# Attention and a gated MoE block on one core: 245 offsets in the plan that orders its work

## The chip, the cores and the metric

The kernel runs on one core of a Trainium2 chip. Its time is the device time of one execution in microseconds. The profile and the trace record one execution on the same core; a time "at 42 us" counts from the first instruction of that execution.

## The reference: what is computed

Eight batches, twelve heads, 448 positions, head size 64. Queries and keys are normalised and scaled by a gain, attention runs without a mask, and the heads side by side (448 x 768 per batch) go through a gated block that mixes positions.

```python
def rmsnorm(x, g):
    return x / np.sqrt(np.mean(x * x, axis=-1, keepdims=True) + 1e-06) * g
q_n, k_n = rmsnorm(q, g_q), rmsnorm(k, g_k)
scores = (1 / np.sqrt(64)) * q_n @ k_n.transpose(0, 1, 3, 2)
attn = np.exp(scores - max)                 # softmax over the keys
x = (attn / sum) @ v                        # -> (8, 448, 768)
h = np.maximum(x @ w_in, 0.0)               # 768 -> 1024
u, v = h[..., :512], h[..., 512:]
v_n = (v - mean(v)) / np.sqrt(var(v) + 1e-06)
v_s = np.einsum('ts,bsd->btd', w_spatial, v_n) + b_spatial[None, :, None]
out = (u * v_s) @ w_out                     # 512 -> 768
```

## The kernel before: tasks, a planner, five engines

The kernel doesn't write its instructions in the order in which they run. It makes a list of 1178 tasks, each with its engine or engines, a duration that the author assumes for each, the tasks it depends on, the buffers it takes and a **position** (`pos`): the smaller, the sooner it is wanted. A planner then walks through assumed time and takes, for one engine after the other, the task that goes next. What comes out is one fixed instruction order per engine; on the chip each engine runs its list strictly in that order and waits where an input or a buffer isn't there yet.

```python
def add(self, *a, **k):
    t = Task(*a, **k)
    ...
    t.pos += self.nudge.get(t.name, 0.0)            # NUDGE["exp G3 r5"]: an offset to the position
    for e in t.costs:
        if f"{t.name} @{e}" in self.nudge:          # NUDGE["relu_u1 b0 @ACT"]: a bias for one engine
            t.bias = {**t.bias, e: self.nudge[f"{t.name} @{e}"]}

# in run(): among the tasks of an engine that could start soon
    for at, t in c:
        if at > first + self.LOOK[e]:
            continue
        if len(t.costs) > 1:                        # two engines can do it: the one that ends first
            mine = at + t.costs[e][1] + t.bias.get(e, 0.0)
            if any(self.start_of(t, o) + t.costs[o][1] + t.bias.get(o, 0.0) < mine - 1e-6
                   for o in t.costs if o != e):
                continue
        s = t.pos + self.WAIT * (at - first)
        if e == "PE" and t.mode != mode:            # TensorE: changing the shape of the array
            s += self.KEEP                          # 0.6; the plan also charges SWITCH = 0.095 for it
        if top is None or (s, at) < top[0]:
            top = ((s, at), t, at)
```

The work comes in 24 groups G (a batch has three: four heads each). Each group is loaded, squared, reduced, scaled, turned (transposed), scored in seven rounds, and each round's scores go through an exponential on ScalarE. From the exponentials TensorE forms the row sums and the values, which VectorE divides into `xt`. When a batch b has its three groups, its gated block runs: `unit_v`, `unit_u`, `unit_s`, `unit_o`. Names as in the plan:

```python
# square{i} G / reduce{i} G / rstd G / scaled{i} G : norm of q (i=0) and k (i=1)
costs = {"POOL": (1.65 * w, ...)}                   # square: GpSimd, and for the first 8 groups
if early: costs["ACT"] = ...; costs["DVE"] = ...    # ScalarE or VectorE as well
# turn{i} G: by TensorE into PSUM for G < 6 (then turned{i} G copies it out, on DVE or ACT);
#            by a transposing DMA from group 6 on (then k_scale G, on DVE or ACT)
# scores [(G, r)]: 8 matmuls of 64x64 tiles, four side by side; blocks of two rounds from G3 on
add(f"scores {blk}", {"PE": ...}, pos, emit, deps=..., get=bufs, mode="S")
# exp G r
act.activation(out=eb.t[:, r], in_=bf.t[:, :, 0:S], func=AF.Exp, bias=0.0, scale=1.0)
# sums G / values0 G / values1 G: matmuls of 128x32 tiles, four side by side, mode "V"
# recip G (ACT: Ln, then Exp), xt0 G / xt1 G (DVE: values times reciprocal)
# w_spT0..3: w_spatial is turned once, by 49 TensorE transposes of 64x64, mode "S"
a = add(f"w_spT{c}", {"PE": (0.7, 1.0)}, 34.0, emit, deps=[wsp_load], get=[bf], mode="S")
# the gated block of batch b; mode "G" (128x128), and "O" for the last 64 positions
add(f"unit_v{c} b{b} {j0}", {"PE": (w, w + 0.26)}, pos, ..., mode="G" if c < 3 else "O")
a = add(f"relu_v{c} b{b}", {"DVE": (0.62, 0.73), "ACT": (0.49, 0.63)}, ...)
# stats{c} b (DVE), ln_rstd b (ACT), ln_apply{c} b (DVE)
# unit_u{f} b -> relu_u{f} b (DVE or ACT);  unit_s{f} b -> gate{f} b (DVE)
# unit_o{c}{h} b -> osb{c}{h} b (DVE or ACT) -> store{c} b (DMA)
```

Until about 25 us the planner also puts dummy matmuls (128x128, results unused) into gaps of TensorE.

Of the kernel before, what the change touches and what calls it, by code (L numbers as in the profile page):

```python
# [225 lines left out]
def kernel(  # L226
# [60 lines left out]

    plan = Planner(tc, NUDGE)
    add = plan.add
# [499 lines left out]


LOG = None
NUDGE = {}


# [28 lines left out]
```

## Time and profile before

| | us |
|---|---|
| time, median of 3 runs (lowest to highest) | 287.81 (287.23 to 288.43) |
| span of the profiled execution | 285.4 |
| TensorE matmul busy | 267.1 |
| ScalarE busy | 217.5 |
| VectorE busy | 209.8 |
| GpSimd busy | 157.2 |

TensorE (PE) is the fullest engine. Of the others ScalarE (ACT) and VectorE (DVE) come next, each about three quarters full over the whole span; over single stretches they are much fuller. The busy time of PE holds stretches in which several matmuls run side by side in different parts of the array, and their ends are modelled, so it says where PE was never empty, not how well it was used. For that, the distance from the start of one matmul to the start of the next is the better measure; the prediction uses it.

### The profile page before, as it was taken

What the parts mean: (1) busy time and instruction counts of PE and PEld (TensorE: products, weight loads), DVE (VectorE), ACT (ScalarE), POOL (GpSimd) and SP (SyncE); (2) the same over time, 40 slices, a digit from 0 to 9 for tenths busy, and PEclk for the clock granted to TensorE, in tenths of its full rate; (3) what the DMA queues carried; (4) which work ended last, traced back from release to release, by engine and by line L of the source; (5) the groups of instructions that cost most, each with busy time, mean ns of one, the idle gap of its engine ahead of it and who ended that gap; (6) DMA issues with size and microseconds to landing.
All of it is one profiled execution on the core that took longest, in us unless ns stands there. A gap on an engine that the chain in (4) does not pass through costs nothing.

```text
span 285.4 us, 7162 instructions
## 1 busy us (share of the span) xinstructions
PE 267.1 (94%) x2870; PEld 124.8 (44%) x2870; DVE 209.8 (74%) x357; ACT 217.5 (76%) x348; POOL 157.2 (55%) x132
## 2 busy tenths in 40 slices
PE   5688979999899999999999999999999999999990
PEld 5443436444344344444444443444443443445550
DVE  1999797889998858878888776874977667452530
ACT  4189984787877898878999887888887978876531
POOL 7533364965786498479888989149871440000011
PEclk9999997999999999999999999999999999999998
DMA  7999598387799978999898899988993562006114
GB/s 253 290 250 223 139 256 209 66 163 198 196 204 245 224 108 218 222 280 208 311 178 204 179 220 244 138 256 192 190 195 32 105 167 54 2 0 165 31 39 155
DMA packets 65379, 50.02 MB, mean 175 GB/s; under 512 B 41985, under 2 KB 61906, under 8 KB 65346
## 3 DMA queue, kind: packets, MB, share of 16 engines
q1 hardware_dynamic: 51266, 40.61, 57.4%
q0 software_dynamic: 14080, 8.96, 23.5%
q8 instruction: 22, 0.36, 0.6%
q14 instruction: 11, 0.09, 0.1%
HBM read 38.55 MB, written 11.01 MB: 174 GB/s over the span
## 4 chain that ended last, share of the span: by engine, by line
PE 66%; issue 19%; DVE 7%; ACT 3%; POOL 2%; POOLq 0%; DVEq 0%
PE pss L550 11%; PE ps L618 10%; PE ps L713 10%; PE ps L660 8%; PE ps L753 7%; PE ps L729 7%; PE ps L597 5%; ACT et L573 2%; PE ps L664 2%; DVE ms L462 2%; DVE sq L449 1%; PE ps L320 1%; DVE nq L483 1%; PE ps L774 1%; POOL nk L483 1%
## 5 line engine op out<-in xcount | busy, mean ns | idle before, releaser
L573 ACT ACTIVATE et<-pss 128x896 bf16<-128x896 f32 x168 | 144.2, 914 | 26.5 <-PE pss L550 25.8
L462 DVE TENSOR_REDUCE ms<-sq 128x14 f32<-128x896 f32 (+1 forms) x50 | 51.3, 1037 | 5.9 <-ACT sq L447 3.8
L550 PE MATMUL pss<-qT,kT 64*64 64x448 bf16 x672 | 51.3, 363 | 3.9 <-ACT et L573 2.5
L483 POOL TENSOR_TENSOR nq<-qf,rs 128x896 bf16<-128x896 f32 x17 | 28.7, 1689 | 39.6 <-ACT rs L470 29.5
L627 DVE TENSOR_TENSOR xt<-ps,rc 128x448 bf16<-128x448 f32 x48 | 29.0, 622 | 20.7 <-ACT rc L606 10.3
L618 PE MATMUL ps<-et,vt 128*32 128x448 bf16 x768 | 41.2, 353 | 0.1
L449 POOL TENSOR_TENSOR sq<-qf 128x896 f32<-128x896 f32 x20 | 33.7, 1685 | 12.2 <-DVE nk L483 4.1
L713 PE MATMUL ps<-xt,w_in 128*128 128x448 bf16 x192 | 39.9, 353 | 0.0
L449 POOL TENSOR_TENSOR sq<-kf 128x896 f32<-128x896 f32 x19 | 32.0, 1686 | 9.1 <-DVE sq L449 4.0
L483 POOL TENSOR_TENSOR nk<-kf,rs 128x896 bf16<-128x896 f32 x20 | 33.8, 1689 | 5.7 <-DVE nq L483 3.4
L660 PE MATMUL ps<-w_in,xt 128*128 128x512 bf16 x144 | 35.3, 384 | 0.1
L753 PE MATMUL ps<-w_out,gt 128*128 128x384 bf16 x192 | 34.7, 327 | 0.5 <-DVE gt L734 0.5
L550 PEld LDWEIGHTS <-kT 64*64 64x64 bf16 x672 | 15.0, 104 | 34.9 <-issue 29.8
L685 DVE BATCH_NORM_STATS2 s<-vs 128x6 f32<-128x512 bf16 (+1 forms) x32 | 22.0, 687 | 9.6 <-ACT vs L635 9.0
L729 PE MATMUL ps<-w_spT,vn 128*128 128x448 bf16 (+1 forms) x128 | 27.6, 354 | 0.0
L618 PEld LDWEIGHTS <-vt 128*32 128x32 bf16 x768 | 19.4, 97 | 18.0 <-issue 5.1
L734 DVE TENSOR_TENSOR gt<-ps,us 128x448 bf16<-128x448 f32 x32 | 19.8, 622 | 9.8 <-PE ps L729 8.5
L765 POOL DMA_DIRECT2D out_dram<-osb x3 | 1.7, 556 | 44.9 <-ACT osb L741 44.9
L713 PEld LDWEIGHTS <-w_in 128*128 128x128 bf16 x192 | 17.3, 98 | 20.6 <-issue 6.4
L375 POOL DMA_DIRECT2D vt<-in_v_dram x32 | 21.6, 683 | 6.2 <-DVE nq L483 3.2
L753 PEld LDWEIGHTS <-gt 128*128 128x128 bf16 x192 | 17.4, 98 | 16.9 <-issue 5.3
L597 PE MATMUL ps<-et,ones 128*32 128x448 bf16 x384 | 23.4, 355 | 0.3 <-ACT et L573 0.3
(69 smaller groups left out, 278.8 us busy)
## 6 DMA issues: line engine op xcount, KB each, us to landing
qf<-in_q_dram SPq DMA_DIRECT2D x24, 448.0 KB, 4.5
kf<-in_k_dram SPq DMA_DIRECT2D x24, 448.0 KB, 5.4
out_dram<-osb SPq DMA_DIRECT2D x45, 192.0 KB, 3.5
vt<-in_v_dram POOLq DMA_DIRECT2D x16, 192.0 KB, 6.6
vt<-in_v_dram POOLq DMA_DIRECT2D x16, 144.0 KB, 6.3
w_in<-in_moe_w_in_dram POOLq DMA_DIRECT2D x2, 768.0 KB, 9.2
out_dram<-osb SPq DMA_DIRECT2D x15, 96.0 KB, 3.2
w_out<-in_moe_w_out_dram POOLq DMA_DIRECT2D x1, 768.0 KB, 9.2
```

What stands on the lines that cost most here:

```text
L449: eng_of[e].tensor_tensor(out=sqb.t[:, h], in0=r.t[:, h], in1=r.t[:, h], op=ALU.mult)
L462: dve.tensor_reduce(out=ms.t[:, i, h], in_=sqb.t[:, h].rearrange("p a (s d) -> p a s d", d=D), axis=AX.X, op=ALU.add)
L483: eng_of[e].tensor_tensor(out=nb.t.rearrange("p s a d -> p a s d")[:, :, s0:s1, :], in0=r.t.rearrange("p a (s d) -> p a s d", d=D)[:, :, s ...
L550: pe.matmul(out=ps[64 * h:64 * h + 64, a, 0:S], lhsT=kb[64 * a:64 * a + 64, slot, 64 * xk:64 * xk + 64], rhs=qb[64 * a:64 * a + 64, :, 64 ...
L573: act.activation(out=eb.t[:, r], in_=bf.t[:, :, 0:S], func=AF.Exp, bias=0.0, scale=1.0)
L597: pe.matmul(out=bf.t[32 * l:32 * l + 32, 0:S], lhsT=ones[:, (0 if c < 3 else 1 + x), :], rhs=eb.t[:, r, a, :], start=(c == 0), stop=(c == ...
L618: pe.matmul(out=bf.t[32 * l:32 * l + 32, 0:S], lhsT=vb.t[:, 2 * (g + 3 * a) + x, c, half::2], rhs=eb.t[:, r, a, :], start=(c == 0), stop=( ...
L627: dve.tensor_tensor(out=xb.t[:, j * S:j * S + S], in0=bf.t[:, 0:S], in1=rc.t, op=ALU.mult)
L660: pe.matmul(out=bf.t, lhsT=xb.t[:, j * S + 128 * c:j * S + 128 * c + 128], rhs=w_in[:, j, DH:DF], start=(j == 0), stop=(j == 5))
L713: pe.matmul(out=bf.t[:, 0:S], lhsT=w_in[:, j, 128 * f:128 * f + 128], rhs=xb.t[:, j * S:j * S + S], start=(j == 0), stop=(j == 5))
L729: pe.matmul(out=bf.t[:, 0:S], lhsT=vn.t[0:kp, c, 128 * f:128 * f + 128], rhs=w_spT[0:kp, c, :], start=(c == 0), stop=(c == 3))
L753: pe.matmul(out=bf.t[:, 0:384], lhsT=gt.t[:, f, 128 * c:128 * c + 128], rhs=w_out[:, f, 384 * h:384 * h + 384], start=(f == 0), stop=(f == 3))
```

## The change

The table of offsets, empty before, is filled: 245 entries, of which 183 move a task's position (from -54 to +84) and 62 bias a task towards or away from one engine. It is the outcome of a search over plans, and it is for a better order of the same work: no task is added, removed or resized, and no result changes its arithmetic other than by the engine that evicts or squares it.

```diff
-NUDGE = {}
+NUDGE = {
+    "unit_o00 b5": 2, "unit_v1 b3 0": 0.3, "relu_u1 b1": 10, "unit_u1 b6": 11, "turn0 G3 0": -16,
...
+    "turned0 G0 0 @DVE": 7, "scores [(15, 2), (15, 3)]": -1, "square1 G4 0 @DVE": 3,
...
+    "values0 G23 0": 9, "values0 G22 0": 18, "unit_u2 b6": 5,
+    "osb00 b1 @ACT": -2, "scaled0 G9 0": 9, "rstd G19": 5, "w_spT1": -18, "values0 G3 0": 7,
...
+    "turn0 G5 0": 66, "sums G4 0": 45, "unit_o3 b4": -22, "exp G19 r0": -3, "reduce1 G10 0": 10,
+    "w_spT2": -54, "scaled1 G2 0": 4, "ln_apply0 b5": 7, "values0 G20 0": 3, "gate1 b0": -18,
...
+    "scaled0 G1 0 @POOL": -9, "square0 G1 0 @DVE": 11, "unit_v2 b5 0": 5.87032,
+    "scores [(13, 2), (13, 3)]": -13, "unit_v0 b0 4": -20, "square1 G10 0": 23,
+}
```

What it does to the order of instructions, read from the two built programs:

| | before | after |
|---|---|---|
| TensorE matmuls, of which dummies | 2869, 95 | 2867, 93 |
| changes of TensorE's array shape between two matmuls | 222 | 236 |
| tasks that change their engine | | 73 |
| `relu_u` on DVE / ACT | 23 / 9 | 15 / 17 |
| `osb` on DVE / ACT | 27 / 29 | 35 / 21 |
| `turned` on DVE / ACT | 14 / 0 | 9 / 5 |
| `scaled` on DVE / POOL | 13 / 37 | 10 / 40 |
| `square` on ACT / DVE / POOL | 5 / 6 / 39 | 7 / 7 / 36 |

Where TensorE meets the first gated block, the order before is: values of group 2, `w_spT0`, two rounds of scores, `w_spT1` to `w_spT3`, the rest of `unit_v0`, `unit_v3`, and on. After it is: `w_spT2` ahead of the last round of group 2, `w_spT1` between its sums, `w_spT0` and `w_spT3` between its values, then `unit_v1`, scores, the rest of `unit_v0` and `unit_v1`, `unit_v3`, `unit_u3`, `unit_v2`, the other `unit_u` with the turns of groups 4 and 5 between them, and only then the last round of group 3.

## The prediction, written before the changed kernel was run

> **What bounds the kernel now.** I read the page's slices of the span first (40 slices of 7.1 us; each digit a busy share in tenths).
>
> ```profile
> PE   5688979999899999999999999999999999999990
> ACT  4189984787877898878999887888887978876531
> PEclk9999997999999999999999999999999999999998
> ```
>
> PE is full from the twelfth slice on. Before that it has an 8 and a 7, ACT is at 9 in slices 4 and 5, and the granted clock dips in slice 7. So there are at least two regimes. Cutting the span at the first exponential, at the first gated block and at the end of group 5's values gives the table of stretches:
>
> ```profile
> 0.00:14.40 14.40, 8.97 (x99) 7.37 (x99) 8.01 (x23) 4.90 (x9) 9.59 (x22) 1.00 1.01 273
> 14.40:42.00 27.60, 23.27 (x327) 11.34 (x327) 25.85 (x31) 25.68 (x39) 10.92 (x12) 1.00 0.95 217
> 42.00:77.20 35.20, 33.81 (x375) 17.17 (x369) 30.48 (x49) 25.65 (x44) 22.30 (x17) 0.95 0.73 169
> 77.20:285.40 208.20, 201.04 (x2082) 88.89 (x2078) 145.50 (x257) 161.26 (x258) 114.39 (x84) 1.00 0.80 164
> ```
>
> (After each stretch and its length: busy us of PE, weight loads, DVE, ACT, POOL; clock; DMA share; GB/s.) From 14.4 to 42 ACT works 25.68 of 27.6 us and DVE 25.85: exponentials and norms set the pace, and PE has too little to do, because no gated block can run before group 2's values. From 77.2 on ACT has 161 of 208 us and PE never rests. What ended PE's waits there is one line of the list of waits, and the same list for 45 to 77.2 has two:
>
> ```profile
> PE ps L753 <- DVE gt L734: 0.5, 2, 0.3
> ...
> PE pss L550 <- ACT kT L527: 0.9, 1, 0.9
> PE ps L597 <- ACT et L573: 0.3, 1, 0.3
> ```
>
> But "never rests" isn't "at its peak". The starts of the matmul records show it: inside a run, 448 columns follow at 189 ns, 512 at 216, 384 at 163; where the array's shape changes, the next start is 282 ns away. PE's timeline shows it in the large:
>
> ```profile
> 99.52 0.57 PE L550 MATMUL pss<-qT,kT 64*64 64x448 bf16 x8
> 100.02 1.47 PE L753 MATMUL ps<-w_out,gt 128*128 128x384 bf16 x8
> 101.43 0.69 PE L550 MATMUL pss<-qT,kT 64*64 64x448 bf16 x8
> ```
>
> Eight score matmuls, four abreast, are 2 x 0.189 = 0.38 us, yet the next run starts 0.50 later. From 77.2 to the last matmul at 278.45 I added up all starts: 201.2 us elapsed; 181.1 us if each matmul took its distance within a run (four or two abreast counted once); 0.56 us in two waits; 161 shape changes. So a change costs (201.2 - 181.1 - 0.56)/161 = **0.122 us**, and 19.6 us of this stretch are changes. From 42 to 77.2 the same sum is 34.9 elapsed, 27.0 streamed, 24 changes at 0.122 = 2.9: **5.0 us lost**, to waits and clock. Where, the timeline tells:
>
> ```profile
> 42.78 2.28 PE L412 MATMUL ps<-ident,w_sp 64*64 64x64 bf16 x35 [0.23 <-DVE xt L627]
> 45.00 1.04 PE L660 MATMUL ps<-w_in,xt 128*128 128x512 bf16 x2
> ...
> 72.82 0.38 PE L550 MATMUL pss<-qT,kT 64*64 64x448 bf16 x4
> 74.09 0.38 PE L550 MATMUL pss<-qT,kT 64*64 64x448 bf16 x4 [0.89 <-ACT kT L527]
> ...
> 45.00:48.30 3.30, 3.30 (x23) 1.90 (x23) 2.30 (x5) 0.76 (x2) 1.69 (x1) 0.50 0.94 302
> ```
>
> While the gated block is ready (xt at 42.7), PE turns w_spatial until 45.0. Then the clock record grants half speed from 44.9 to 48.3, so the first matmuls of the block take twice their time: 1.7 us lost. At 72.8 to 75.4 scores wait for a k_scale on ACT, and sums for an exponential: 1.4 us.
>
> **What the Trainium skill says.** "TensorE: Matmul & The Clock Gate", Part 1, section "What's actually happening": the clock is halved or full, decided over free-running windows of 3.4 us by how busy PE was. The trace agrees: the half-speed record lasts 3.413 us and follows a window of short transposes with a 1.4 us gap. Its Part 4 says that transposes don't count as busy in the same way; that suits this place, though no run so far separates transposes from the gap. The section "Back-to-back issue gap" gives N/2.4 + 2.5 ns, 189.2 for 448 columns: 189 here. None of the three states the price of a shape change; the 0.122 is this trace's. "Perfetto Trace Analysis", section "Identifying the Most-Contended Engine", warns that matmul busy time misleads; here it reads 100% over a stretch with a tenth of it in changes.
>
> **The change part by part.**
>
> (1) *Start.* The square of k of group 1 moves from DVE (1.08 us, from 9.35 to 10.43) to ACT, and the first piece of the turned q of group 0 (0.42 us on DVE) moves to ACT. DVE scales group 0 as soon as ACT has its factor (10.05 instead of 10.35), and its chain of copies to the first scores is 0.42 shorter: first exponential 0.3 + 0.42 = **0.7 us** earlier, about 13.6.
>
> (2) *14 to 42 us.* ACT gets one more copy (a turned q of group 3, about 0.9 us by its 0.914 us for an exponential of 896 columns), DVE loses work. ACT stays the bound, and with 1.9 us of idle time in 27.6 there is little to win. I take group 2's values as ready at the same 42 us, or up to 0.7 earlier.
>
> (3) *w_spatial.* Its 49 transposes, 57 ns apart, are 2.8 us. About 40 of them stand after 42 us now. In the order after, all four tasks stand ahead of group 2's last values, between scores that wait for ACT. That takes **2.3 us** out of the full stretch, and spreads them so that a half-speed window becomes unlikely: **1.7 us**.
>
> (4) *First gated block.* PE does unit_u of batch 0 ahead of the last round of group 3, while ACT takes their four evictions (0.545 each), four turned copies and a square. Counted from the lists of tasks up to the last exponential of group 5, ACT gains 7.3 us of work and gives away 4.4 (k_scale, three osb, a relu_v3, two rstd): 3 us more. From 14.4 to 75.35 it now works 49.5 and idles 11.5, so it fits. In the order after, k_scale of group 6 is DVE's: the 1.4 us of waits at 73 should shrink; I count **0.7**.
>
> (5) *Shape changes.* 222 become 236. Up to the round that begins group 6 there are 5 more of them between tasks (56 for 51), where PE partly waits anyhow, and 7 more after it: 7 x 0.122 = **0.9 us lost**.
>
> (6) *The rest.* After 77 us there are only 0.56 us of waits to save. Last matmul to end of span (278.45 to 285.4) is one eviction on ACT and the last store; both stay: 0. DVE gets the osb back and sheds relu_u; neither engine bounds there.
>
> Sum if all goes well: -0.7 - 2.3 - 1.7 - 0.7 + 0.9 = -4.5 us, and -5.5 with the rest of the waits gone. The bound by PE agrees: streamed work after 42 us is 27.0 - 2.3 + 181.1 = 205.8, with some 196 changes at 0.122 = 23.9; from 41.5 that ends at 271.2, with 7.0 of tail a span of 278.2, or 7.2 less. No plan of many in-order lists reaches a bound of no wait at all. I take 80% of the 4.5, because the moved values and scores of groups 3 to 5 sit close to their exponentials: **-3.6 us**, 284.2.
>
> **Rivals.** *ACT becomes the bound in 44 to 77 us.* It is given 3 us, and six exponentials of 0.914 us sit behind evictions that PE itself waits for through four PSUM buffers. For it: ACT was at nine tenths before 42. Against it: 11.5 us of idle time. If it comes, parts 3 and 4 shrink to about half: -1.5, some 286.3. *A late stage that runs without waits now loses that.* Positions were moved by up to 36 far beyond batch 0, with no wait there to remove; values and first matmuls of the last block now follow each other directly. Every displaced pair could add a few tenths, 1 to 3 us in all: about 286. For it: the plan works with assumed durations; against it: the same durations gave a plan with 0.56 us of waits in 200. *Shape changes eat it.* With waits no smaller, 14 x 0.122 = 1.7 us slower, 289.5. Against it: the transposes visibly leave the full stretch. *More than I see.* The bound allows -7.2, 280.6, if the start and the waits vanish together.
>
> **Range and chances.** The parts are worth 1 to 6 us together; the rivals take up to 3. That gives 281.6 to 287.8 around **284.2**. Two per cent faster is 282.05, which needs nearly all of the bound: 0.17. Two per cent slower is 293.6, six us of new waits in a stage that has none: 0.02.
>
> **What would show it.** In the profile after: first exponential near 13.6; no w_sp transposes after the first unit_v of the full stretch, and clock 1.00 between 40 and 50 us; PE full from about 42; the last values of group 5 done three to four us before 77.2; from there on 201 us plus about 0.9 to the last matmul, and a tail of 7. It would be wrong if PE shows new waits for ACT or DVE after 77, if a half-speed window falls elsewhere, or if group 2's values come later than 42.

## The result, and the profile after

| | before | after |
|---|---|---|
| time, median (lowest to highest), us | 287.52 (287.18 to 288.43) | 284.31 (283.93 to 285.10) |
| ratio to before, 95% interval | | 0.9887 (0.9854 to 0.9920) |
| span of the profiled execution, us | 285.4 | 282.2 |

The change is 1.1% faster, about 3.2 us, and 284.31 stands beside 284.2 predicted. The page's slices of the span of the changed kernel, 7.05 us each:

```profile
PE   5788999899999999999999999999999999999990
ACT  4399998889977899798799889987887888773521
PEclk9999999999999999999999999999999999999997
```

The 7 in PE's sixth slice and the dip of the clock in the seventh are gone, and ACT stays at 8 or 9 in slices 6 and 7, where before it fell to 8 and 4. The stretches, cut at the same events as before (first exponential, first matmul of the gated block behind group 2's values, just behind the last values of group 5); after each stretch come the busy us of PE, weight loads, DVE, ACT and POOL, the clock, the DMA share and GB/s:

```profile
0.00:14.24 14.24, 9.45 (x95) 7.88 (x95) 6.92 (x21) 6.14 (x11) 9.51 (x22) 1.00 1.01 272
14.24:41.10 26.86, 24.33 (x354) 13.38 (x353) 23.96 (x30) 25.39 (x38) 15.73 (x14) 1.00 0.87 209
41.10:74.70 33.60, 32.39 (x356) 15.26 (x354) 29.62 (x47) 30.16 (x48) 17.66 (x13) 1.00 0.87 198
74.70:282.20 207.50, 199.58 (x2060) 88.20 (x2066) 146.67 (x252) 161.04 (x263) 115.54 (x84) 0.99 0.76 163
```

In the third stretch ACT now works 30.2 of 33.6 us; before it was 25.7 of 35.2. What ended PE's waits in that stretch, in the list of waits (us in total, times, longest):

```profile
PE pss L550 <- ACT qT L508: 0.9, 1, 0.9
PE pss L550 <- ACT et L573: 0.2, 1, 0.2
```

One wait for a copy on ACT has taken the place of another: 1.1 us here, 1.2 before. The wait for k_scale at 74 us is gone; the new one, for the turned q of group 4, ends at 53 us. PE's timeline where w_spatial is turned (L412) and the gated block begins (L660):

```profile
34.05 0.61 PE L412 MATMUL ps<-ident,w_sp 64*64 64x64 bf16 x10
...
35.66 0.91 PE L412 MATMUL ps<-ident,w_sp 64*64 64x64 bf16 x14
...
38.07 1.43 PE L412 MATMUL ps<-ident,w_sp 64*64 64x64 bf16 x19
...
41.13 1.04 PE L660 MATMUL ps<-w_in,xt 128*128 128x512 bf16 x3
...
42.60 1.04 PE L660 MATMUL ps<-w_in,xt 128*128 128x512 bf16 x4
```

The transposes are over when the block can go on: at 41.13 come matmuls that need only groups 0 and 1 (before has such at 30.96 already), and at 42.60 the first that need group 2, which before started at 45.00. The profile lacks eleven of the 144 matmul records of L660; gaps of 0.44 us between two of those are such holes and no waits.

For what follows I split every profile at three events: first exponential; start of the last values matmul of group 5; start of the last matmul. The first varies by a microsecond between profiles that start with the same instructions (14.24, 15.11 and 15.37 in three of them, 14.36 to 14.57 in five others), so the second column, counted from it, compares better than the span. What varies is the landing of a small transfer, the gains: in `after` VectorE's product of the gains starts behind it at 6.91 us, in w_spatial_back at 7.83 and in head_after at 8.09. In `after`, `tail_after` and the versions built on after, two rounds of scores of group 6 (0.50 us with their change of shape) fall ahead of the second event and not behind it.

| profile, us | first exponential | to group 5's last values | from there to the last matmul | to the end |
|---|---|---|---|---|
| before | 14.36 | 62.60 | 201.49 | 6.95 |
| after | 14.24 | 59.42 | 201.59 | 6.90 |
| head_after | 15.37 | 60.26 | 201.48 | 7.00 |
| tail_after | 14.37 | 63.22 | 201.34 | 6.82 |
| w_spatial_moved | 14.48 | 63.09 | 201.49 | 7.02 |
| w_spatial_by_matmul | 14.57 | 62.87 | 201.49 | 7.06 |
| w_spatial_back | 15.11 | 61.75 | 201.57 | 7.37 |
| engines_only | 15.78 | 69.69 | 201.30 | 6.99 |
| order_only | 15.57 | 68.87 | 201.57 | 6.76 |
| gains_later_before | 14.15 | 62.66 | 201.49 | 7.25 |
| k_scale_on_vector | 14.52 | 63.80 | 201.62 | 7.03 |
| gains_later | 12.55 | 59.50 | 201.56 | 7.02 |
| turns_sooner | 12.99 | 59.63 | 201.60 | 6.89 |
| turns_sooner_tail_before | 12.37 | 61.67 | 202.58 | 7.37 |

So the difference of 3.25 us between the two spans is 0.12 at the start, **3.18 between 14 and 77 us**, -0.10 in the 200 us after that, and 0.05 at the end. Counted at equal work, with the 0.50 us of the two rounds put back, it is 3.7 us gained up to group 5 and **0.6 us given back** in the late stage.

### The profile page after: what moved, and what is told of

The parts are those of the page before. It is cut to its first block, busy times and chain, and to the rows that moved or that the text cites. A ratio compares the mean times of both kernels' runs of the same rounds, so it can differ in the third digit from the quotient of the medians.

```text
span 282.2 us, 7121 instructions
## 1 busy us (share of the span) xinstructions
PE 265.8 (94%) x2857; PEld 124.7 (44%) x2868; DVE 207.2 (73%) x348; ACT 222.7 (79%) x357; POOL 158.4 (56%) x132
## 4 chain that ended last, share of the span: by engine, by line
PE 81%; ACT 7%; DVE 7%; POOL 2%; issue 2%; POOLq 0%; DVEq 0%; ACTq 0%
PE pss L550 14%; PE ps L753 12%; PE ps L618 11%; PE ps L660 10%; PE ps L713 10%; PE ps L729 9%; PE ps L597 7%; ACT et L573 4%; PE ps L664 2%; PE ps L774 2%; PE ps L320 2%; DVE s L685 1%; DVE nq L483 1%; PE ps L412 1%; DVE ms L462 1%
## 5 line engine op out<-in xcount | busy, mean ns | idle before, releaser
L483 POOL TENSOR_TENSOR nk<-kf,rs 128x896 bf16<-128x896 f32 x22 | 38.0, 1730 | 16.6 <-ACT rs L470 8.0
L618 PE MATMUL ps<-et,vt 128*32 128x448 bf16 x768 | 42.8, 354 | 0.0
L483 POOL TENSOR_TENSOR nq<-qf,rs 128x896 bf16<-128x896 f32 x18 | 30.4, 1692 | 17.8 <-ACT rs L470 8.0
L449 POOL TENSOR_TENSOR sq<-qf 128x896 f32<-128x896 f32 x18 | 30.3, 1684 | 13.2 <-DVE kT L529 8.1
L753 PE MATMUL ps<-w_out,gt 128*128 128x384 bf16 x192 | 35.2, 327 | 0.3 <-DVE gt L734 0.3
L660 PE MATMUL ps<-w_in,xt 128*128 128x512 bf16 x133 | 33.6, 380 | 1.0 <-issue 0.6
L449 POOL TENSOR_TENSOR sq<-kf 128x896 f32<-128x896 f32 x18 | 30.3, 1682 | 3.4 <-DVE ms L462 2.8
L765 POOL DMA_DIRECT2D out_dram<-osb x3 | 1.7, 557 | 48.3 <-ACT osb L741 48.3
L743 DVE COPY osb<-ps 128x384 f32<-128x384 f32 x35 | 18.6, 553 | 11.5 <-PE ps L753 11.1
```

The source lines that it names most:

```text
L449: eng_of[e].tensor_tensor(out=sqb.t[:, h], in0=r.t[:, h], in1=r.t[:, h], op=ALU.mult)
L483: eng_of[e].tensor_tensor(out=nb.t.rearrange("p s a d -> p a s d")[:, :, s0:s1, :], in0=r.t.rearrange("p a (s d) -> p a s d", d=D)[:, :, s ...
L618: pe.matmul(out=bf.t[32 * l:32 * l + 32, 0:S], lhsT=vb.t[:, 2 * (g + 3 * a) + x, c, half::2], rhs=eb.t[:, r, a, :], start=(c == 0), stop=( ...
L660: pe.matmul(out=bf.t, lhsT=xb.t[:, j * S + 128 * c:j * S + 128 * c + 128], rhs=w_in[:, j, DH:DF], start=(j == 0), stop=(j == 5))
L753: pe.matmul(out=bf.t[:, 0:384], lhsT=gt.t[:, f, 128 * c:128 * c + 128], rhs=w_out[:, f, 384 * h:384 * h + 384], start=(f == 0), stop=(f == 3))
```

## The experiments

With the offsets alone one can't try a part of the change: taking two of the 245 away makes the planner choose anew far behind. In the experiments the planner chooses nothing. It walks down a list of pairs (engine, task), written out from the order before or after, and each diff below is a diff of that list. Line numbers in these kernels stand 21 lower than in before and after.

```diff
-        for _ in range(len(self.tasks)):
-            ...                                # weigh the tasks, take the best
+        for e0, name in ORDER:                 # ("PE", "g2 col"), ("PE", "turn0 G0 0"), ...
+            at, e, t = self.start_of(named[name], e0), e0, named[name]
```

### Head or tail

**head_after**: the list of after up to the round that begins group 6, then the list of before for what is left.

> The order after up to the round that begins group 6 (to about 73 us), then the order before for all that is left; 219 changes of the array's shape between tasks instead of 226. Theory (the head carries the gain, 3.8 us at equal work, and the late moves cost 0.6): 283.7 us, the span from the last values of group 5 to the last matmul about 201.1. Rival (the late moves are needed to take up what the new head leaves behind): new waits of TensorE after 74 us, 285 to 286 us.

Measured 285.55 us, ratio 0.9899 (0.9874 to 0.9924): the head has nearly all of the gain. The 285.55 lies in the rival's range. Of the new waits that it named there is one, at 74.1 us at the joint, that neither order has (window 60 to 285 us of the list of waits):

```profile
PE ps L576 <- ACT et L552: 0.8, 1, 0.8
```

Behind it the third column is that of before (201.48), so the new head doesn't need the late moves. This profile also starts 1.1 us later than `after`, with the gains.

**tail_after**: the reverse, before up to that round, then after.

> The order before up to the same round, then the order after. Theory: 0.4 to 0.8 us slower than before, 288.1 us, for 7 more changes of the array's shape at 0.122 us. Rival (the late part holds a gain of its own): 287 us or less.

Measured 287.97, ratio 1.0003 (0.9988 to 1.0019). The late moves bring nothing, and cost less than expected: by the interval -0.3 to +0.5 us. The profile has 0.47 from the first exponential to the last matmul (264.56 for 264.09), within it.

### Moving w_spatial

**w_spatial_moved**: before, with eight tasks moved, and `bias` on DVE with them, right ahead of w_spT2's copy.

```diff
+PE  w_spT2          (ahead of scores (2,6); copies on DVE behind each)
+PE  w_spT1          (ahead of the second part of the sums of group 2)
+PE  w_spT0, w_spT3  (between the values of group 2)
-PE  w_spT0 ... w_spT3 (behind the values of group 2)
```

> The order before on every engine, with only the four tasks that turn w_spatial on TensorE, and their copies on VectorE, put where the order after has them, into the gaps between scores and values of group 2. Theory (2.3 us of transposes leave the full stretch and the half-speed window goes with them, 1.7 us): 283.8 to 285 us, clock 1.00 from 40 to 50 us. Rival (the gain is in the order of the first gated block and its evictions on ScalarE): at most 1 us faster, 286.5 to 287.5 us.

Measured 288.94, ratio 1.0031 (1.0014 to 1.0048): **slower**, and both expectations missed. The clock is full from 40 to 50 us, as the theory said. PE's timeline has the reason:

```profile
37.11 0.75 PE L576 MATMUL ps<-et,ones 128*32 128x448 bf16 x12 [0.84 <-DVE w_spT L397]
...
40.12 0.94 PE L597 MATMUL ps<-et,vt 128*32 128x448 bf16 x16 [0.77 <-DVE w_spT L397]
...
43.40 0.94 PE L597 MATMUL ps<-et,vt 128*32 128x448 bf16 x16 [0.47 <-DVE w_spT L397]
...
47.40 0.56 PE L478 MATMUL ps<-ident,nq 128*128 128x128 bf16 x7 [1.01 <-DVE nq L462]
...
49.23 0.56 PE L478 MATMUL ps<-ident,nk 128*128 128x128 bf16 x7 [0.83 <-ACT lnms L448]
```

The sums and values wait for a PSUM buffer that the copies of w_spatial free. The first two of these copies stand in DVE's list behind other work (`bias`, 0.95 us; a reduction and a square) while their transposes are done; the third follows its transposes at once. The gaps of PE were there, but DVE, 25.85 of 27.6 us full, had little room for what PE put into them. The last two waits, 1.84 us, are for the scaled q and k of group 4 (the second is listed under ACT, but GpSimd scales this k until 49.18). The scaling of q on DVE starts at 45.09 us for 44.04 in before, and takes 2.25 us for 1.08; a square on GpSimd ran beside its first 1.3 us, but whether that stretched it isn't shown. From unit_v3's first matmul to the scores at 73 us, at full clock, it is 27.89 us, where before takes 26.86 with 2.32 us of half speed in it. So this run gave back the clock's gain as well as that of the transposes.

**w_spatial_back**: the other way, after with these eight tasks put where before has them.

> The order after on every engine, with only the four tasks that turn w_spatial, and their copies, put back to where they stood before: behind the values of group 2, around the first matmuls of the gated block. Theory (in the order after they cost nothing and here they stand in the full stretch): 2.3 us slower than after, and up to 1.7 more if the half-speed window comes with them: 286.5 to 288 us. Rival (TensorE isn't what bounds the head, as moving them alone brought nothing): within 1 us of after, 284.3 to 285.3 us.

Measured 286.44, ratio 0.9970 (0.9951 to 0.9988), against 0.9887 of after: 0.83% or 2.4 us slower, and in the profile 2.33 us to group 5 (61.75 for 59.42). The 2.3 us of the expectation are there to the tenth, but that is partly luck: they were reckoned for some 40 transposes, and here all 49 stand in the full stretch again and take 3.0 us:

```profile
43.15 1.54 PE L391 MATMUL ps<-ident,w_sp 64*64 64x64 bf16 x28
44.62 1.04 PE L639 MATMUL ps<-w_in,xt 128*128 128x512 bf16 x4
45.59 1.63 PE L391 MATMUL ps<-ident,w_sp 64*64 64x64 bf16 x21
```

The clock record of this profile is at full speed until PE's work ends, so the half-speed window has no part in these 2.3 us, and 49 transposes in two rows need not bring it.

### The half-speed window

**w_spatial_by_matmul**: before, each transpose an ordinary matmul.

```diff
-pe.matmul(out=ps[64*y:64*y+64, t, 0:64], lhsT=x, rhs=ident[0:64, 0:64], is_transpose=True, ...)
+pe.matmul(out=ps[64*y:64*y+64, t, :], lhsT=x, rhs=ident[0:64, 0:64], start=True, stop=True)
```

> The order before, with the 49 transposes of w_spatial done as ordinary matmuls with the identity (float32 into PSUM), so that every instruction keeps its place. Theory (transposes don't count as work for the clock): no half-speed window at 45 us, 1.5 us faster, 286.0 us. Rival (the gap of 1.4 us ahead of them lowers the clock): the half-speed window stays, 287.5 us within 0.3.

Measured 287.81, ratio 1.0003 (0.9980 to 1.0026): no difference. The window didn't go; the clock record holds half speed for twice as long, from 42.0 to 48.9 us. So it isn't the kind of instruction, at least not alone. That the longer window cost only some 0.3 us (62.87 for 62.60) fits its place: its first half lies over the w_spatial matmuls, 64 columns each, which follow one another in pairs every 0.10 us here at half speed as in before at full speed.

What the window costs where PE is full came out of another run, **k_scale_on_vector**, which was made for the wait at 73 us: before, with k_scale of group 6 on DVE.

```diff
-("ACT", "k_scale G6"),
+("DVE", "k_scale G6"),
```

> The order before, with one task on another engine: k_scale of group 6 on VectorE, behind the last eviction of batch 0, instead of on ScalarE. Theory (this copy is what scores wait for at 73 us): 0.7 to 1.0 us faster than before. Rival (the sums behind it wait for the exponential of group 5 anyhow, and VectorE then delays the scaling of group 7): within 0.3 us of before.

Measured 288.10, ratio 0.9993 (0.9971 to 1.0015): no gain, as the rival said. The wait only changed its name:

```profile
74.12 0.38 PE L529 MATMUL pss<-qT,kT 64*64 64x448 bf16 x4
75.90 0.38 PE L529 MATMUL pss<-qT,kT 64*64 64x448 bf16 x4 [1.40 <-DVE kT L508]
```

In this profile half speed lasted longer. The stretch from 44.2 to 51.0 us of this run, and then of before:

```profile
44.20:51.00 6.80, 6.80 (x44) 4.00 (x43) 5.73 (x12) 1.79 (x5) 2.39 (x2) 0.50 0.62 178
```

```profile
44.20:51.00 6.80, 6.80 (x52) 4.11 (x51) 5.73 (x11) 2.27 (x6) 2.72 (x2) 0.75 0.61 177
```

PE's order is the same in both, and it doesn't rest in them; 44 matmuls were done instead of 52. From the first matmul of unit_v3 to the scores at 73 us it took 28.20 us (45.92 to 74.12) for 26.86 (45.96 to 72.82): 1.34 us more, for 5.05 us of half speed instead of 2.32. Half of the difference is 1.36. The other three profiles with before's order on PE here (tail_after, w_spatial_by_matmul, gains_later_before; 2.32 to 2.51 us of half speed) fit: less half of that time, all five take 25.67 to 25.70 us. So a half-speed window costs **half its length where PE is full**; of before's, 45.0 to 48.3 us lay there: 1.65 us, nearly the 1.7 of the prediction.

All five profiles have half speed at this place, for 3.4 or 6.8 us; of those with after's order and engines none has. Each profile is one execution, though: over the 22 of w_spatial_back the mean clock lies between 0.975 and 0.996, so some of them must have had windows that its profile lacks. What sets a window off stays open. In before the transposes follow a wait of 1.06 us (1.41 from the last values' start to theirs):

```profile
41.26 0.60 PE L412 MATMUL ps<-ident,w_sp 64*64 64x64 bf16 x9 [1.06 <-DVE xt L627]
```

In w_spatial_back the transposes are there, this wait isn't, and the clock stays up, which points to the wait. But a wait alone isn't enough: the 1.40 us at 75.9 us in k_scale_on_vector and the five of 0.47 to 1.01 us in w_spatial_moved brought no window. (Four profiles also have one between 12.8 and 20.3 us, where the dummies run; what those cost wasn't measured.)

### Engines or order

In the head 26 tasks change their engine. **engines_only**: before's sequence, with these 26 on their new engines. **order_only**: after's sequence, with these 26 on their old ones.

> Every engine's tasks in the sequence before, but the 26 tasks of the head (to the round that begins group 6) that the change gives to another engine stand on that engine. TensorE's order is that of before to the last matmul. Theory (VectorE with its strict list holds up TensorE's turns and the first gated block, and 6.4 us less work there is what lets the head shrink): 285 to 286 us, half or more of the gain. Rival (the order on TensorE is the gain): 287 to 288.5 us.

> The sequence after on every engine, but the same 26 tasks of the head stand on the engine they had before. Theory (VectorE's load is what matters): the order alone makes TensorE wait for copies and evictions on VectorE, 287 to 290 us. Rival (the order is the gain): 284.5 to 285.5 us.

Measured 295.67, ratio 1.0269 (1.0223 to 1.0314), and 292.45, ratio 1.0170 (1.0123 to 1.0216). Both theories of a single cause fall: **each half alone makes the kernel slower, by 2.7% and 1.7%; together they make it 1.1% faster.** PE's list of waits from 14 to 90 us, of engines_only and then of order_only:

```profile
PE ps L478 <- POOL nk L462: 2.1, 2, 1.8
PE pss L529 <- DVE kT L508: 1.8, 1, 1.8
```

```profile
PE pss L529 <- ACT et L552: 2.8, 7, 0.7
PE pss L529 <- DVE qT L489: 2.1, 2, 1.7
```

Scalings that went to POOL without an earlier place arrive late at the turn; copies left on DVE in an order that counts on ACT arrive late at the scores. In both profiles there are half-speed windows too (engines_only has three after 30 us, order_only two of 6.8 us), four of the five behind a wait of 1.2 to 1.8 us. Where a wait brings one, it costs more than its own length; how the 7 us of engines_only divide between waits and clock isn't measured. Order_only took 291.3 us in an execution with a mean clock of 0.997 as well, so most of its loss isn't the clock.

### The start

**gains_later**: after, with the product of the gains behind the reductions of group 0.

```diff
 DVE reduce0 G0 0
-DVE g2, g2 copy
 DVE reduce1 G0 0, reduce0 G0 1, reduce1 G0 1
+DVE g2
 DVE scaled0 G0 0 ... scaled1 G0 1
+DVE g2 copy
```

> The order after, with one more move: VectorE computes the product of the two gains after the four reductions of group 0, and copies its column after the four scalings, where both stood ahead of three of these reductions and made them wait for the gains' transfer. Theory (the reductions then end at 7.4 us and not at 9.6, and ScalarE bounds what follows): the first exponential at about 12.2 us and not 14.2, and 1.5 to 2 us faster than after, 282.5 us. Rival (the loads of groups 1 and 2 or of the weights take over as the bound): the first exponential comes earlier, but group 2's values don't; 284 us.

Measured 282.31, ratio 0.9818 (0.9786 to 0.9850), against 0.9887 of after: 2.0 us faster, **the best version of this study** together with turns_sooner. DVE's timeline in after, and then in this run:

```profile
6.91 0.28 DVE L350 SCALAR_TENSOR_TENSOR g_row<-g_row 1x128 f32<-1x128 f32 x1 [1.35 <-DMA g_row<-in_g_k_dram]
7.91 0.16 DVE L361 COPY g_col<-ps 128x1 f32<-128x1 f32 x1 [0.72 <-PE ps L357]
7.98 1.66 DVE L462 TENSOR_REDUCE ms<-sq 128x7 f32<-128x448 f32 x3
```

```profile
6.25 1.67 DVE L441 TENSOR_REDUCE ms<-sq 128x7 f32<-128x448 f32 x3 [0.56 <-ACT sq L426]
7.84 0.27 DVE L329 SCALAR_TENSOR_TENSOR g_row<-g_row 1x128 f32<-1x128 f32 x1
```

In after, three reductions whose inputs are there at 6.6 us stand behind two small instructions that wait for a transfer of 0.5 KB. Moved, they run 1.7 us sooner, and so does the first exponential (12.55 for 14.24); nothing gives it back later. It is the same transfer whose landing moves the start of the profiles by a microsecond.

**gains_later_before**: the same move in before.

> The order before, with only the product of the gains and its copy moved behind the reductions and scalings of group 0. Theory (the start has its bound in the transfer of the gains, whatever stands behind it): first exponential near 12.6 instead of 14.4 us and 1.7 us faster than before, 286.1 us. Rival (the order before gives the time back, because ScalarE or VectorE sets group 2's values): 287 to 287.9 us.

Measured 287.40, ratio 0.9973 (0.9952 to 0.9994): 0.2 to 1.4 us faster by the interval, and 0.21 in the profile's first column. The reductions ended just as early, but DVE's next instruction was the square of group 1's k:

```profile
9.07 1.09 DVE L428 TENSOR_TENSOR sq<-kf 128x896 f32<-128x896 f32 x1 [1.09 <-DMA kf<-in_k_dram]
10.08 1.15 DVE L462 TENSOR_TENSOR nq<-qf,rs 128x512 bf16<-128x512 f32 x2
```

Two hurdles stand one behind the other in DVE's list, the gains and this square. The change takes the second away and gains 0.1 us, this move takes the first away and gains 0.2; both together gain 1.8 (14.36 to 12.55).

### Two more steps

**turns_sooner**: gains_later, with `turn0 G4` and `turn0 G5` ahead of `unit_u2 b0` on PE, and `turned0 G4` two places up on ACT.

> The version with the gains moved (282.3 us), and TensorE turns q of groups 4 and 5 ahead of the last unit_u of batch 0, with ScalarE's copy of group 4's ahead of its two evictions. Theory (the wait of 1.24 us at 50.4 us, for that copy, disappears behind unit_u): 0.9 us faster, 281.4 us. Rival (VectorE's scalings aren't ready sooner, or ScalarE bounds up to group 5): no change, 282.3 us.

Measured 282.92, ratio 0.9805 (0.9777 to 0.9834): not to be told from gains_later. The wait of 0.9 us for that copy went; two shorter ones came, of 0.4 and 0.3 us, one of 0.2 stayed, and the column to group 5 is 59.63 for 59.50.

**turns_sooner_tail_before**: turns_sooner up to the round that begins group 8, then the list of before.

> The version of turns_sooner up to the round that begins group 8, then the order before; 218 changes of the array's shape between tasks instead of 226. Theory (each change costs 0.122 us): 0.5 to 1.0 us faster than turns_sooner, about 280.8 us. Rival (as where the tail before was joined at group 6, the joint costs a wait of about the same size): no gain, 281.4 us.

Measured 284.04, ratio 0.9852 (0.9819 to 0.9884): slower than turns_sooner by 0.5%. The third column is 1.0 us longer, where eight changes of shape should have saved as much. The list has 0.7 us more of PE's waits there, 0.5 of it at the joint; the rest isn't traced. In this profile, the slowest of the six executions (286.11), DVE also waited 2.2 us for a load of k in the head, in an order that is the same as in turns_sooner. How often that happens, one profile can't tell.

## Why the prediction was right, step by step

The number was right to 0.1 us, and part of that is luck: 284.2 was 3.6 below the 287.81 known then, and the gain measured against 287.52 is 3.2. Its parts were not all right; the discount at the end covered the two that were too high.

- **Regimes.** The bound by PE after the first block and by ACT and DVE before it holds: from group 5's last values to the last matmul both take 201.5 us, 0.6 apart at equal work. "Sum up the starts, subtract what streams" gave 0.122 us for a change of shape; in after the same sum for this stretch gives 0.122 too, with nine matmuls of L660 added whose records are missing. One sum of mine was wrong: of the 27.0 us that stream between 42 and 77.2, only 0.5 are transposes, and taking off 2.3 for them takes off 1.8 too much. The bound is then 5.4 us less than before and not 7.2, and of the "5.0 us lost, to waits and clock" 1.7 are neither: they are the rest of the 2.2 us that 35 transposes took.
- **Part 1, the start: 0.7 predicted, 0.12 measured.** The failed step is "its chain of copies is 0.42 shorter" together with the 0.3. I read DVE's chain from the factor on and left out what set the factor itself: the reductions behind the gains' transfer. They began 0.2 us later in this profile (7.98 for 7.78), so the scaling began at 10.29 and not at 10.05 (10.35 before). And the copy that went to ACT brought 0.08 and not 0.42: k's first copy starts at 12.95 for 13.09, because it has TensorE's turn of k to wait for, which ends at 12.92. Even the 0.12 can't be told from the scatter of the gains' landing. gains_later shows what the start was worth.
- **Part 2.** "The same 42 us, or up to 0.7 earlier" holds for what the block waits for: group 2's `xt` is done at 42.3 us for 42.7. Its last values matmul starts a microsecond later than in before (40.84 for 39.85), with the transposes now ahead of it.
- **Part 3: 2.3 and 1.7 predicted.** 2.33 in w_spatial_back, for more transposes than I counted; the window is gone, and its price is half its length, 1.65. Both sizes hold, the second as a price and not as a gain that a run showed by itself. What I had wrong was that this is a change on its own: w_spatial_moved loses 0.9 us.
- **Part 4: 0.7 of waits predicted, 0.1 measured** (1.2 to 1.1 us). The failed step is that I counted the wait that goes and not one that comes. The wait for k_scale did go in after. But TensorE turns the q of group 4 only at 51.1 us, ACT has a part of the layer norm and an eviction ahead of its copy (52.26 to 53.17), and the scores wait 0.9 us; when turns_sooner took that wait away, two others came. The engine of k_scale alone decides nothing: in k_scale_on_vector the transposed k had landed by 72.5 us, but the copy stood in DVE's list behind the last eviction and ran at 74.78.
- **Part 5: 0.9 lost predicted;** -0.3 to +0.5 by tail_after, and 0.6 in the profile of after at equal work. The five more in the late stretch in the built programs' matmuls (166 for 161) would be 0.6.
- **The 80%** was a guess at what in-order lists give back. The 4.5 was 5.4 of gains (start 0.7, transposes 2.3, clock 1.7, waits 0.7) less 0.9 for changes of shape. The runs have 0.1, 2.3, 1.65 and 0.1: 4.2, or 1.2 less. With the 0.6 that the late stage gave back that is 3.6, where the two spans differ by 3.25; the head has five more changes of shape as well, which would be 0.6, but what took the last 0.3 isn't shown. So the mechanism held, two terms were mis-sized, and the discount of 0.9 stood in for them; that it fitted so closely is luck.
- **Rivals.** ACT got its 3 us and more (30.2 us of 33.6 in the third stretch), but PE's waits for it stayed at 1.1 us. New waits of the late stage did not come (0.3 us in after, 0.5 before). The bound without any wait isn't reached; the 1.7 us of the start, of which it counted 0.5, show that more was open.

## What to carry to other kernels

This plan of five in-order lists couldn't be credited item by item: moving work to another engine and moving it in the order paid only together, and each alone cost more than both gained, so judge such a change by regimes and test it by swapping whole stretches. Before counting a gap of the fullest engine as room, look whether the engine that must take its results has room at the same time. At the start of a kernel, ask of every in-order list which instruction waits for a transfer while later ones have their inputs: two such instructions in a row hide each other's price.

## What the runs showed of the hardware

TensorE's half-speed windows came in one or two units of 3.4 us, at different times in executions of the same order: in the five profiles with before's order they begin between 41.3 and 44.9 us. Nine of the ten windows between 30 and 90 us in all profiles began 0.3 to 3.6 us behind a wait of 1.05 to 1.84 us; a wait of 1.40 us in k_scale_on_vector brought none. Each us of half speed cost 0.5 us where TensorE was full (1.34 us for 2.73 more us of it). Replacing 49 transposes of 64 columns by ordinary matmuls did not keep the clock up.
